# The last 64 keys of an attention chunk: eighth of thirteen slots, one score product, VectorE alone

## The chip, the cores and the metric

The kernel runs on one core of one Trainium2 chip. TensorE (PE in the profile) multiplies, VectorE (DVE), ScalarE (ACT) and GpSimd (POOL) work on elements, and SyncE (SP) issues most DMAs. PEld is TensorE's loading of weights, which overlaps its products. The metric is the time of one execution in device microseconds, the median of three runs.

## The reference

For eight batches of S = 3136 tokens, an attention with squared rectified scores, multiplied by `u`, and then a routed feed-forward layer on 128 tokens of each batch:

```python
scale = 1.0 / S
scores = scale * np.matmul(z, z.transpose(0, 2, 1))     # z: (8, 3136, 64)
attn = np.maximum(scores, 0.0) ** 2
x = u * np.matmul(attn, v)                              # v: (8, 3136, 256)
...
for b in range(B):                                      # routed layer, capacity 128
    top_idx = np.argpartition(-(x[b] @ w_gate), capacity)[:capacity]
    xe = x[b, top_idx]
    ye = np.maximum(xe @ w1, 0.0) @ w2
    out[b, top_idx] = xe + sigmoid(gate)[:, None] * ye
```

## The kernel before

**Precision.** Products run on a reduced form of fp32, so that each operand is kept as a high part, a rounded copy, and a low part, what the rounding left. `ZH` and `ZL` hold the parts of z, with 64 rows of features twice over the 128 partitions; `V` holds both parts of v. `Z[b, c]` is the moving operand of the scores: the high part of a chunk's z on partitions 0 to 63, the low part on the others. So a product with `ZH` and one with `ZL` add up to the full score.

**Chunks and slots.** A batch's queries are cut into seven chunks: five of 512 columns (`c < WHOLE`), one of 256 and one of 320. The keys of a chunk are 24 tiles of 128 and a rest of 64. A slot takes two tiles (a pair), so a chunk has 12 pair slots and one slot for the rest, the thirteenth and last. The list `slots` fixes their order. The scores are symmetric: tiles of squares that an earlier chunk computed are stored transposed to DRAM (`turned` in `low`, tiles `aT`, `squares`) and fetched again (`qk`); such a slot is "old" and needs no score products.

**One slot.** `scores(k)` is issued three slots ahead (`LEAD`): four products of scores for a new pair, into one of two PSUM buffers `sc`. ScalarE rectifies into `a` (L450) and squares into the high part `hi` (L451). The exact square is made on VectorE (L462) or ScalarE (L456), whichever the planner's account (`busy`, `spend`) sees as freer. `low(k)` makes the difference `lo` on VectorE or GpSimd (L518) and, where the tile is wanted later, transposes on VectorE (L483). `mix(k)` then adds twelve products into two PSUM sums `acc` (h = 0 and 1): eight with `hi` and four with `lo`. In the first slot of a chunk they are sorted by sum. Where in the twelve the scores of slot k + 3 are issued is `turn`.

**The rest slot.** The columns of `ZH` and `ZL` behind the 24 tiles hold the last 64 keys twice, so the scores come out twice, on partitions 0 to 63 and 64 to 127. On the lower half `hi` keeps the high part; on the upper half VectorE multiplies (L462, 64x512) and takes the difference (L474). With `hi` holding the high part above the low part, four products with `Vr`, the rest of v twice over, do the whole sum.

**Around a chunk's end.** `finish` queues two readings of the sums on VectorE (L601), transposes and the store of the output. Three PSUM buffers serve the two sums, so the second sum of a new chunk waits for the first reading. The choice of the routed tokens (`route`) and the feed-forward layer (`expert`) of the batch before are cut into tasks that are mixed into later pair slots; on VectorE most of them fall into the second and third chunk of the next batch. In the last batch the last four chunks (`LATE`) are handled by another scheme.

**Order.** Each engine runs its instructions in the order of the program; the schedule is written out by hand.

## Time and profile before

| | |
|---|---|
| median of 3 runs | 2067.78 us (2067.12 to 2067.83) |
| the profiled execution | 2067.41 us |
| its span, first to last instruction | 2065.6 us |
| TensorE busy | 2055.2 us (99%) |
| VectorE, ScalarE, GpSimd busy | 1529.0 us (74%), 1291.2 us (63%), 1357.5 us (66%) |
| granted TensorE clock | 1.0 of full speed |

The median is that of whole executions; the span is measured inside one execution, and some 1.8 us lie around it. Busy times of the engines overlap, so they do not add up to the span. A matmul's busy time in the records covers its whole passage and overlaps the next one; how fast products follow each other is read from their starts.

### The profile page before, as it was taken

The page shows a single profiled execution, that of the slowest core. Times are in us where ns is not written, and L with a number is a line of the kernel's source. Part 1 is how long each engine was busy: PE and PEld are TensorE (multiplying, and loading weights), DVE is VectorE, ACT ScalarE, POOL GpSimd, SP SyncE. Part 2 cuts the span into 40 slices and gives each one's busy share as a digit, 9 for nine tenths or more (in the row PEclk, how much of TensorE's full clock was granted, in tenths as well). Part 3 has the DMA queues.
Part 4 walks back from the last instruction along what each step waited for, and adds up shares of the span by engine and source line. Part 5 has one row for each costly group of instructions (what it writes and reads, how often), then busy time and mean ns, then how long its engine had stood idle before and what let it go on. Part 6 is the DMA issues. An engine that isn't in the chain of part 4 may idle for free.

```text
span 2065.6 us, 31660 instructions
## 1 busy us (share of the span) xinstructions
PE 2055.2 (99%) x10280; PEld 1744.5 (84%) x10280; DVE 1529.0 (74%) x2667; ACT 1291.2 (63%) x1629; POOL 1357.5 (66%) x728
## 2 busy tenths in 40 slices
PE   9999999999999999999999999999999999999999
PEld 6888988889888898888988889888898888888788
DVE  7676678856788667875678756887578876787776
ACT  7665576656775467664676546765477654775543
POOL 6766587756876468764677647875578755765643
PEclk9999999999999999999999999999999999999999
DMA  6788767886668765787767877678776776666862
GB/s 197 207 232 226 217 188 207 233 231 190 193 188 232 212 205 177 199 233 210 208 185 193 235 203 217 184 192 236 194 222 188 192 201 178 206 192 164 213 173 95
DMA packets 442758, 415.52 MB, mean 201 GB/s; under 512 B 133792, under 2 KB 374880, under 8 KB 439520
## 3 DMA queue, kind: packets, MB, share of 16 engines
q1 hardware_dynamic: 441456, 411.01, 70.9%
q0 software_dynamic: 768, 2.10, 0.3%
q8 instruction: 80, 1.31, 0.3%
q14 instruction: 86, 0.70, 0.1%
q10 hardware_dynamic: 368, 0.39, 0.1%
HBM read 238.78 MB, written 174.60 MB: 200 GB/s over the span
## 4 chain that ended last, share of the span: by engine, by line
PE 87%; DVE 3%; issue 2%; ACT 2%; DMA 2%; POOL 1%; SPq 1%; POOLq 0%; DVEq 0%; ACTq 0%
PE acc L556 73%; PE sc L440 12%; ACT hi L451 1%; POOL lo L518 1%; ACT a L450 1%; DVE a L462 1%; DVE aT L483 1%; PE h L1215 1%; PE y L1259 1%; DMA vst<-in_v 0%; DMA squares<-aT 0%; DVE lo L518 0%; DMA qk<-in_zt 0%; PE spread L680 0%; DMA qk<-squares_narrow 0%
## 5 line engine op out<-in xcount | busy, mean ns | idle before, releaser
L556 PE MATMUL acc<-hi,V 128*128 128x512 f32 (+2 forms) x5376 | 1218.4, 364 | 0.5
L518 POOL TENSOR_TENSOR lo<-a,hi 128x1024 fp32r<-128x1024 f32 (+2 forms) x326 | 717.9, 2204 | 563.5 <-DVE a L462 426.7
L556 PEld LDWEIGHTS acc<-hi,V 128*128 128x128 f32 x5376 | 932.9, 188 | 157.4 <-DVE ut L601 5.5
L556 PE MATMUL acc<-lo,V 128*128 128x512 f32 (+2 forms) x2688 | 664.0, 363 | 1.0 <-POOL lo L518 1.0
L450 ACT ACTIVATE a<-sc 128x1024 f32<-128x1024 f32 (+4 forms) x401 | 358.2, 893 | 449.2 <-PE sc L440 421.0
L556 PEld LDWEIGHTS acc<-lo,V 128*128 128x128 f32 x2688 | 471.1, 188 | 76.7 <-POOL lo L518 4.4
L462 DVE TENSOR_TENSOR a<-sc,a 128x1024 f32<-128x1024 f32 (+5 forms) x306 | 307.4, 1005 | 249.8 <-ACT hi L451 225.8
L418 ACT CAST hi<-qk 128x1024 fp32r<-128x1024 f32 (+2 forms) x327 | 279.7, 860 | 220.1 <-PE acc L556 198.1
L483 DVE STREAM_TRANSPOSE aT<-a 128x512 f32<-128x512 f32 (+3 forms) x541 | 349.5, 681 | 76.7 <-ACT a L456 54.4
L451 ACT ACTIVATE hi<-a 128x1024 fp32r<-128x1024 f32 (+4 forms) x401 | 372.2, 928 | 24.8 <-PE acc L556 2.3
L518 DVE TENSOR_TENSOR lo<-qk,hi 128x1024 fp32r<-128x1024 f32 (+2 forms) x220 | 319.2, 1459 | 81.7 <-ACT hi L418 79.3
L440 PE MATMUL sc<-Z,ZH 128*128 128x512 f32 (+2 forms) x746 | 275.1, 373 | 2.3 <-DVE a L462 2.1
L440 PE MATMUL sc<-Z,ZL 128*128 128x512 f32 (+2 forms) x746 | 273.3, 370 | 0.1
L518 POOL TENSOR_TENSOR lo<-qk,hi 128x1024 fp32r<-128x1024 f32 (+2 forms) x107 | 210.0, 1965 | 51.3 <-ACT hi L418 41.6
L440 PEld LDWEIGHTS sc<-Z,ZH 128*128 128x128 f32 x746 | 140.5, 188 | 31.7 <-DVE a L462 6.0
L440 PEld LDWEIGHTS sc<-Z,ZL 128*128 128x128 f32 x746 | 140.5, 188 | 24.7 <-DVE ZL L126 0.5
L126 POOL TENSOR_TENSOR V<-vst,V 128x512 fp32r<-128x512 f32 x92 | 136.5, 1489 | 29.8 <-ACT V L125 26.4
L622 POOL TENSOR_TENSOR ut<-x,w_run 128x1024 f32<-128x1024 f32 (+2 forms) x52 | 126.0, 2422 | 24.4 <-DVE x L613 23.4
L456 ACT ACTIVATE a<-a 128x1024 f32<-128x1024 f32 x93 | 98.8, 1062 | 2.9
L126 POOL TENSOR_TENSOR ZL<-zst,ZH 128x512 fp32r<-128x512 f32 (+2 forms) x56 | 84.2, 1508 | 2.5 <-ACT ZH L125 2.2
L125 ACT CAST V<-vst 128x512 fp32r<-128x512 f32 x95 | 57.9, 609 | 35.5 <-DMA vst<-in_v 35.5
L601 DVE SCALAR_TENSOR_TENSOR ut<-acc,ut 128x512 f32<-128x512 f32 (+2 forms) x112 | 63.9, 611 | 19.5 <-PE acc L556 19.2
(187 smaller groups left out, 1083.1 us busy)
## 6 DMA issues: line engine op xcount, KB each, us to landing
squares<-aT SPq DMA_DIRECT2D x160, 512.0 KB
qk<-squares SPq DMA_DIRECT2D x320, 256.0 KB
squares_narrow<-aT SPq DMA_DIRECT2D x320, 128.0 KB
qk<-squares_narrow SPq DMA_DIRECT2D x80, 512.0 KB
out<-x SPq DMA_DIRECT2D x162, 128.0 KB
ut<-in_ut SPq DMA_DIRECT2D x40, 512.0 KB
vst<-in_v SPq DMA_DIRECT2D x158, 128.0 KB
squares_own<-aT SPq DMA_DIRECT2D x39, 256.0 KB
```

What stands on the lines that cost most here:

```text
L126: (lo_on or nc.vector.tensor_tensor)(lo, src, hi.bitcast(F32), op=ALU.subtract)
L418: nc.scalar.copy(by(hi), src)
L440: nc.tensor.matmul(ps[:, q], z[:, j * P : (j + 1) * P], mov, start=z is ZH, stop=z is ZL)
L450: nc.scalar.activation(a, ps[:, :n], AF.Relu)
L451: nc.scalar.activation(pieces[0][0](hi), pieces[0][1], AF.Square)
L456: nc.scalar.activation(a, a, AF.Square)
L462: square = lambda: nc.vector.tensor_tensor(a[rows], of[rows, :n], a[rows], op=ALU.mult)
L483: nc.vector.transpose(to, a[rows, q].rearrange("p (m t a) -> p m t a", m=GT, a=Q))
L518: on.tensor_tensor(view(lo), src, view(hi).bitcast(F32), op=ALU.subtract)
L556: nc.tensor.matmul(ac[h], w, mov, start=first and h not in started, stop=stop)
L601: nc.vector.scalar_tensor_tensor(xT[:, h, :w], acc[b, c][h], SCALE * SCALE, xT[:, h, :w], op0=ALU.mult, op1=ALU.mult)
L622: nc.gpsimd.tensor_tensor(wx, runs, consts["wg_run"].rearrange("p (o r) -> p o r", o=1).broadcast_to([P, NB, RUN]), op=ALU.mult,)
```

## The change

The last 64 keys' slot moves from the end of a chunk to the eighth place (`MIDDLE`), in the chunks that `inside` names: all but the first of a batch, and in the last batch only the second and third, 44 of 56. There the new `rest_scores` is used. For all chunks the columns of the last keys are laid out anew: `ZH` holds their high parts and then their low parts side by side, `ZL` the reverse. One product with `ZH` then gives the high part's score on partitions 0 to 63 and the low part's on 64 to 127; ScalarE copies the latter down, and VectorE adds, rectifies and squares, rounds to `hi` and takes the difference. The products of other chunks still use both. Because a pair's slot is now the last of such a chunk, it stops the accumulation and has its products sorted by sum.

```diff
@@ -106,6 +106,7 @@
     ROUNDS = 32 // BITS
     SHARES = P >> BITS
     SLOTS = NJ // 2 + 1
+    MIDDLE = SLOTS // 2 + 1
 
     const = ctx.enter_context(tc.tile_pool(name="const", bufs=1))
     vpool = ctx.enter_context(tc.tile_pool(name="vpool", bufs=NJ // 2))
@@ -251,7 +252,9 @@
         on = on or (nc.gpsimd.tensor_tensor if b else None)
         split(src, by_rows(ZH, a, m), by_rows(ZL, a, m), hi_on, lo_on=on)
         if m < n:
-            split(staged["z", b, of][:, o + m : o + n], ZH[:, a + m : a + n], ZL[:, a + m : a + n], lo_on=on)
+            e = a + m + 64
+            for q, (hi, lo) in enumerate(((ZH[:, a + m : e], ZL[:, a + m : e]), (ZL[:, e : a + n], ZH[:, e : a + n]))):
+                split(staged["z", b, of][:, o + m + q * 64 :][:, :64], hi, lo, lo_on=on)
         spend(pool=0.65 + 0.0017 * n if b else 0.0)
 
     def bring_z(b, c):
@@ -316,6 +319,10 @@
 
 
 
+    def inside(b, c):
+
+        return c > 0 and c < (NCH if b < B - 1 else NCH - LATE)
+
     slots = []
     for b in range(B):
         for c in range(NCH):
@@ -333,8 +340,9 @@
             if b < B - 1 and c == NCH - 1:
                 place = [1.6 / len(old)]
             both += [(x, 1, js, False) for x, js in zip(place, new)]
-            slots += [(b, c, js, is_old) for _, _, js, is_old in sorted(both)]
-            slots.append((b, c, (NJ,), False))
+            mine = [(b, c, js, is_old) for _, _, js, is_old in sorted(both)]
+            mine.insert(MIDDLE if inside(b, c) else len(mine), (b, c, (NJ,), False))
+            slots += mine
     assert len(slots) == B * NCH * SLOTS
 
     squares = [
@@ -433,6 +441,8 @@
         if is_second(k):
             mov, w = mov.rearrange("p (f x) -> p f x", x=P)[:, :, P // 2 :], w // 2
         ps = ps_s.tile([P, 2, CH], F32, name="sc", tag="sc")[:, :, :w]
+        if n == 1 and inside(b, c):
+            return rest_scores(k, ps[:, 0], mov)
         todo = [(q, j, z) for q, j in enumerate(js) for z in (ZH, ZL)]
         if k < 2:
             todo.sort(key=lambda x: x[2] is ZL)
@@ -463,15 +473,35 @@
             spend(act=2 * act, dve=dve)
         lows.append((k, a, hi, pieces, square))
 
+    def rest_scores(k, ps, mov):
+
+        b, c, js, _ = slots[k]
+        w = CHUNKS[c][1]
+        nc.tensor.matmul(ps, ZH[:, NJ * P :], mov, start=True, stop=True)
+        both = work.tile([P, 2, CH], F32, name="a", tag="a", bufs=3)[:64, :, :w]
+        hi = work.tile([P, 2, CH], F32R, name="hi", tag="hi2", bufs=LEAD)[:, :1, :w]
+        a, s = both[:, 0], both[:, 1]
+        nc.scalar.copy(s, ps[64:])
+        spend(act=0.13 + 0.0008 * w)
+
+        def square():
+            nc.vector.tensor_tensor(s, ps[:64], s, op=ALU.add)
+            nc.vector.scalar_tensor_tensor(a, s, 0.0, s, op0=ALU.max, op1=ALU.mult)
+            nc.vector.tensor_copy(hi[:64, 0], a)
+            spend(dve=0.3 + 0.0026 * w)
+
+        lows.append((k, both[:, :1], hi, [], square))
+
     def low(k, a, hi, pieces, square):
 
         b, c, js, is_old = slots[k]
         c0, w = CHUNKS[c]
         n = len(js)
         lo = None
-        rows = slice(0, P) if n == 2 else slice(64, P)
+        one = n == 1 and inside(b, c)
+        rows = slice(0, P) if n == 2 else slice(0, 64) if one else slice(64, P)
         if n == 1:
-            nc.vector.tensor_tensor(hi[rows], a[rows], hi[rows].bitcast(F32), op=ALU.subtract)
+            nc.vector.tensor_tensor(hi[64:], a[rows], hi[rows].bitcast(F32), op=ALU.subtract)
             spend(dve=0.05 + 0.001 * w)
         def turned():
             if turns(k):
@@ -489,11 +519,11 @@
                     stores.append(lambda: nc.sync.dma_start(to, t.rearrange("p m q x -> p m (q x)")))
                 else:
                     f0 = q0 // 2 * GT if c < WHOLE else 0
-                    for f in range(GT) if n == 2 else (2, 3):
+                    for f in range(GT) if n == 2 else range(2) if one else (2, 3):
                         if n == 2:
                             to = narrow[f0 + f]
                         else:
-                            to = narrow[2 * GT if c < WHOLE else GT, :, :, (f - 2) * x : (f - 1) * x]
+                            to = narrow[2 * GT if c < WHOLE else GT, :, :, f % 2 * x : (f % 2 + 1) * x]
                         src = t[f * Q : (f + 1) * Q, :, :n].rearrange("a m q x -> a m (q x)")
                         stores.append(lambda to=to, src=src: nc.sync.dma_start(to.rearrange("m a x -> a m x"), src))
             elif is_first(k):
@@ -529,15 +559,15 @@
         b, c, js, _ = slots[k]
         assert k in parts
         hi, lo = parts.pop(k)
-        first, last = k % SLOTS == 0, js[0] == NJ
+        first, last, rest = k % SLOTS == 0, k % SLOTS == SLOTS - 1, js[0] == NJ
         if first:
             acc[b, c] = [ps_a.tile([P, CH], F32, name="acc", tag="acc")[:, : CHUNKS[c][1]] for _ in range(NK)]
         ac = acc[b, c]
         todo = []
-        if last:
+        if rest:
             for h in range(NK):
                 for w in range(2):
-                    todo.append((h, V[b, NJ][:, w, h], hi[:, 0], w == 1))
+                    todo.append((h, V[b, NJ][:, w, h], hi[:, 0], last and w == 1))
         else:
             for h in range(NK):
                 for q, j in enumerate(js):
@@ -545,10 +575,10 @@
                         todo.append((h, V[b, j][:, w, h], hi[:, q], False))
             for q, j in enumerate(js):
                 for h in range(NK):
-                    todo.append((h, V[b, j][:, 0, h], lo[:, q], False))
-            if first and (b or c):
+                    todo.append((h, V[b, j][:, 0, h], lo[:, q], last and q == 1))
+            if first and (b or c) or last:
                 todo.sort(key=lambda x: x[0])
-        turn = (6 if c else 4) if first else 4 if last or len(slots[min(k + 1, len(slots) - 1)][2]) == 1 else 8
+        turn = (6 if c else 4) if first else 4 if rest or len(slots[min(k + 1, len(slots) - 1)][2]) == 1 else 8
         done, lead, started = 0, 2, set()
         for n, (h, w, mov, stop) in enumerate(todo):
             if n == turn:
@@ -559,9 +589,9 @@
             for op in beside[done:upto]:
                 op()
             done = max(done, upto)
+        if last:
+            near.extend(finish(b, c))
         if turn == len(todo):
-            if last:
-                near.extend(finish(b, c))
             between()
 
     gate = {}
@@ -1499,7 +1529,7 @@
         now = settle_scores
         posts = [*posts[:half], now, *posts[half:]]
         held_posts = []
-        if k + 2 < len(slots) and len(slots[k + 1][2]) == 1:
+        if k + 2 < len(slots) and len(slots[k + 1][2]) == 1 and not inside(b, c):
 
             now = square_scores if c < WHOLE and (b or c) else settle_scores
             posts, held_posts = [now], [fn for fn in posts if fn is not settle_scores]
@@ -1515,7 +1545,7 @@
         clock += took
         if tasks:
             ready = max(told + 0.5, clock + 2.0)
-        if len(js) == 1 and cap > 0:
+        if k % SLOTS == SLOTS - 1 and cap > 0:
             if c == NCH - 1 - late:
                 far.extend([None, *route(b)])
             elif c >= NCH - late:
```

The order of the instructions shows where this lands. First TensorE in the second chunk of the fourth batch, before: from the two score products of the last keys, which the tenth slot issues, to their own slot at the end of the chunk. `sc` are score products, `acc` the sums; `Vr` marks the slot of the last keys.

```order
L440 MATMUL sc<-Z,ZH 128x512
L440 MATMUL sc<-Z,ZL 128x512
L556 MATMUL acc<-lo,V 128x512 x4
L556 MATMUL acc<-hi,V 128x512 x8
L440 MATMUL sc<-Z,ZH 128x512
L440 MATMUL sc<-Z,ZL 128x512
L440 MATMUL sc<-Z,ZH 128x512
L440 MATMUL sc<-Z,ZL 128x512
L556 MATMUL acc<-lo,V 128x512 x4
L556 MATMUL acc<-hi,V 128x512 x8
L556 MATMUL acc<-lo,V 128x512 x4
L556 MATMUL acc<-hi,Vr 128x512 x4
```

Two products of scores are followed by what is left of one slot, by two more slots and then by the slot of the last keys. The same chunk after the change, from the products of the fifth slot to the slot of the last keys, the eighth:

```order
L586 MATMUL acc<-hi,V 128x512 x8
L480 MATMUL sc<-Z,ZH 128x512
L586 MATMUL acc<-lo,V 128x512 x4
L586 MATMUL acc<-hi,V 128x512 x8
L450 MATMUL sc<-Z,ZH 128x512
L450 MATMUL sc<-Z,ZL 128x512
L450 MATMUL sc<-Z,ZH 128x512
L450 MATMUL sc<-Z,ZL 128x512
L586 MATMUL acc<-lo,V 128x512 x4
L586 MATMUL acc<-hi,V 128x512 x8
L586 MATMUL acc<-lo,V 128x512 x4
L586 MATMUL acc<-hi,Vr 128x512 x4
```

One product stands where two did, three slots ahead of the four products with `Vr`, which now have pair slots on both sides.

VectorE in the same chunk, before: the middle of the chunk, where the fifth slot's work is, with steps of the routing (`ge`, `tot`, `mi`, `base`) between transposes (`aT`) and a difference.

```order
L808 TENSOR_SCALAR ge,own<-gates,least 128x392
L814 STREAM_TRANSPOSE ge<-own 32x32 x4
L483 STREAM_TRANSPOSE aT<-a 128x4x128 x2
L518 TENSOR_TENSOR lo<-qk,hi 128x1024
L631 TENSOR_REDUCE gate<-ut 128x16
L820 TENSOR_REDUCE tot<-ge 32x16
```

Nothing of the last keys stands here; their multiply and difference come at the end of the chunk. After the change, the same place:

```order
L838 TENSOR_SCALAR ge,own<-gates,least 128x392
L844 STREAM_TRANSPOSE ge<-own 32x32 x4
L488 TENSOR_TENSOR a<-sc,a 64x512
L489 SCALAR_TENSOR_TENSOR a<-a 64x512
L490 CAST hi<-a 64x512
L504 TENSOR_TENSOR hi<-a,hi 64x512
L513 STREAM_TRANSPOSE aT<-a 64x4x128
L513 STREAM_TRANSPOSE aT<-a 128x4x128 x2
L661 TENSOR_REDUCE gate<-ut 128x16
```

The four operations on the last keys and their transpose stand in mid-chunk behind the routing's small transposes, and the difference `lo` that stood there is no longer VectorE's.

## Rows read from the trace of the kernel before

**Rows 1.** The page: span, busy time by engine, the chain that ended last.

```profile
span 2065.6 us, 31660 instructions
PE 2055.2 (99%) x10280; PEld 1744.5 (84%) x10280; DVE 1529.0 (74%) x2667; ACT 1291.2 (63%) x1629; POOL 1357.5 (66%) x728
...
PE 87%; DVE 3%; issue 2%; ACT 2%; DMA 2%; POOL 1%; SPq 1%; POOLq 0%; DVEq 0%; ACTq 0%
```

**Rows 2.** Timeline, TensorE, second chunk of batch four: start us, length us, what.

```profile
821.84 1.98 PE L556 MATMUL acc<-hi,V 128*128 128x512 f32 x8
...
829.09 1.98 PE L556 MATMUL acc<-hi,V 128*128 128x512 f32 x8
830.90 0.39 PE L440 MATMUL sc<-Z,ZH 128*128 128x512 f32 x1
...
832.72 1.98 PE L556 MATMUL acc<-hi,V 128*128 128x512 f32 x8
```

**Rows 3.** Timeline, TensorE, in the chunks of 256 and of 320 columns.

```profile
981.98 1.12 PE L556 MATMUL acc<-hi,V 128*128 128x256 f32 x8
...
988.70 0.64 PE L556 MATMUL acc<-lo,V 128*128 128x256 f32 x4
...
1001.39 1.34 PE L556 MATMUL acc<-hi,V 128*128 128x320 f32 x8
...
1004.91 1.34 PE L556 MATMUL acc<-hi,V 128*128 128x320 f32 x8
```

**Rows 4.** Waits of TensorE's weight loads, whole run: us in total, times, longest.

```profile
PEld sc L440 <- DVE a L462: 6.0, 12, 1.6
PEld acc L556 <- DVE ut L601: 5.5, 13, 0.5
PEld acc L556 <- POOL lo L518: 4.4, 12, 1.1
```

**Rows 5.** Windows: second, third and fourth chunk of batch four.

```profile
core 0: us, PE busy (x) PEld busy (x) DVE busy (x) ACT busy (x) POOL busy (x), PEclk, DMA share, GB/s
...
814.57:856.34 41.77, 41.77 (x188) 34.57 (x186) 39.70 (x96) 29.70 (x32) 29.03 (x15) 1.00 0.59 174
856.34:897.79 41.45, 41.45 (x187) 33.88 (x186) 34.60 (x90) 27.38 (x30) 30.60 (x15) 1.00 0.70 190
897.79:939.90 42.11, 42.11 (x190) 34.79 (x189) 26.69 (x37) 23.43 (x28) 23.62 (x11) 1.00 0.93 250
```

**Rows 6.** Groups by shape: count, busy us, mean ns of one, idle before.

```profile
L462 DVE TENSOR_TENSOR a<-sc,a 128x1024 f32<-128x1024 f32 x186 | 227.3, 1222 | 191.5 <-ACT hi L451 169.3 <-issue 20.9
L518 DVE TENSOR_TENSOR lo<-qk,hi 128x1024 fp32r<-128x1024 f32 x107 | 198.4, 1854 | 14.1 <-ACT hi L418 13.9
...
L474 DVE TENSOR_TENSOR hi<-a,hi 64x512 fp32r<-64x512 f32 x40 | 33.5, 837 | 2.6
...
L462 DVE TENSOR_TENSOR a<-sc,a 64x512 f32<-64x512 f32 x40 | 27.8, 695 | 19.2 <-ACT hi L451 18.1
...
L462 DVE TENSOR_TENSOR a<-a 128x1024 f32<-128x1024 f32 x2 | 2.4, 1222 | 0.4 <-ACT hi L451 0.4
...
L125 DVE CAST ZH<-qk 128x512 fp32r<-128x512 f32 x1 | 0.4, 429 | 0.8 <-DMA qk<-in_zt 0.8
...
L451 ACT ACTIVATE hi<-a 128x512 fp32r<-128x512 f32 x95 | 60.1, 633 | 5.7 <-PE acc L556 0.2
...
L684 ACT COPY row<-spread 128x512 f32<-128x512 f32 x2 | 1.2, 579 | 0.0
```

**Rows 7.** Timeline, VectorE: mid-chunk in the second and third chunk of batch four.

```profile
834.10 0.84 DVE L814 STREAM_TRANSPOSE ge<-own 32x32 f32<-32x32 f32 x4
...
876.87 0.86 DVE L842 TENSOR_SCALAR least<-k_sb,base 32x1 int32<-32x1 int32 x4
878.94 1.23 DVE L462 TENSOR_TENSOR a<-sc,a 128x1024 f32<-128x1024 f32 x1 [1.21 <-ACT hi L451]
```

**Rows 8.** Source L474, the difference for the last keys: ns min/median/max.

```profile
L474 DVE TENSOR_TENSOR hi<-a,hi x56: 422/691/2678, 52.3 to 2037.2; 64x512 fp32r<-64x512 f32 x40, 64x256 fp32r<-64x256 f32 x8, 64x320 fp32r<-64x320 f32 x8
```

## The prediction

> **What bounds the kernel now.** I read the page first. TensorE is busy for 2055.2 of 2065.6 us at the full granted clock, and most of the chain that ended last is its products [rows 1]. A busy TensorE can still lose time between overlapping records, so the next question is the cadence. In the timeline of one chunk (the second of the fourth batch) three slots of 16 products each, all with 512 columns, start at 821.84 and end at 832.72: 10.88 us for 48, so one product costs 0.2267 us when nothing is late [rows 2]. Likewise 56 products with 256 columns take 6.72 us, 0.120 each, and 24 with 320 columns take 3.52 us, 0.147 each [rows 3]. The list of waits says how much of the span is not cadence: weight loads waited 6.0 us for the squares on VectorE, 5.5 for its reading of the sums and 4.4 for a difference on GpSimd, over the whole run [rows 4]. By stage, the windows show TensorE busy without a gap in the chunks around this one, while VectorE is busy for 39.70 of 41.77 us in the second chunk, 34.60 of 41.45 in the third and 26.69 of 42.11 in the fourth [rows 5]. So a product that is taken away is time gained, as long as the engines that feed TensorE stay ahead; VectorE has the least room, in the second chunk of a batch.
>
> **The change part by part.** *The product removed.* In 44 of 56 chunks the last keys need one product where they needed two: 30 chunks of 512 columns, 7 of 256 and 7 of 320 (batches one to seven, all chunks but the first; the last batch, its second and third chunk). The order has exactly that many fewer products with ZL. At the cadences above: 30 x 0.2267 = 6.80, 7 x 0.120 = 0.84, 7 x 0.147 = 1.03, together 8.67 us [rows 2, 3]. This lies on the path, as TensorE waits for almost nothing.
>
> By the Trainium skill (TensorE: Matmul & The Clock Gate, Back-to-back issue gap) an isolated product at full clock takes its columns at 2.4 GHz and 2.5 ns more, 215.8, 109.2 and 135.8 ns here, which would make the sum 8.2 us. The trace's spacing is some 11 ns wider for each, and I use the trace.
>
> *ScalarE* loses a rectification and a square and gets one copy: 0.633 us less for 512 columns, with the copy priced by the copy of another row, 0.579 us [rows 6]. It is not what TensorE waits for; nothing is counted.
>
> *VectorE* did a multiply (0.695 us) and a difference (0.837 us) for these keys. Now it adds (as the multiply, one input still in PSUM: 0.695), rectifies and squares in one instruction, rounds and subtracts. The squaring with both inputs in SBUF lies between half of the in-place square of 1024 columns, 0.61, and the difference's 0.837; I take 0.69. The rounding is like the cast of 128x512, 0.43 [rows 6]. So the chain for 512 columns is 0.695 + 0.69 + 0.43 + 0.837 = 2.65 us where it was 1.53, some 1.1 us more a chunk, at most 44 x 1.1 = 49 us. The planner's own accounts shift too. Counted over the order, 23 squares of pairs go from ScalarE to VectorE (23 x 1.222 = 28 us), and 12 differences of 1024 columns leave it for GpSimd (12 x 1.854 = 22 us) [rows 6]. VectorE's 1529.0 us become about 1585, 77% of the span. In the second chunk of a batch one of those differences leaves, so its load stays near 39.70 + 1.1 + 0.6 - 1.85 = 39.6 us of 41.5. All of this is hidden behind TensorE unless it makes an operand late; then TensorE waits for the difference.
>
> *Is the moved operand late?* In the second chunk, slot 4 (counted from 0) starts at 829.09 [rows 2]. With the new order, slot 4 has 12 products and the one score, 13 x 0.2267 = 2.95 us; slot 5 has 16, 3.63; slot 6 has 12, 2.72: the slot of the last keys starts at 829.09 + 9.30 = 838.39. On VectorE the chain stands right behind the four small transposes that end at 834.94 [rows 7], and the score of these keys is there from 830.9 + 0.4 and copied well before. 834.94 + 2.65 = 837.6, 0.8 us ahead. In the third chunk, slots 4, 5 and 6 before are such that slot 7 comes at 880.4; the last operation ahead of the chain ends at 877.73 with all that stood before it [rows 7], of which one square of 1.22 us is now on ScalarE at that place: 876.5 + 2.65 = 879.2, 1.2 us ahead. The other chunks have VectorE idle for a third of the time. I count 0 for this wait. Its bounds are 0 and, if the two instructions with both inputs in SBUF each took the longest that such a difference took, 2.68 us instead of 0.69 [rows 8], 4.0 - 0.8 = 3.2 us in each of 12 chunks, 38 us. I stay at the near end, since the median of these differences is 0.69 us.
>
> *The end of a chunk* is now a pair's slot, with products sorted by half of the sums. VectorE can read the first sum six products earlier than the end (1.36 us) instead of two (0.45), which can remove up to the 5.5 us of waits for that reading; on the other hand the differences are needed after four products rather than eight, as in the first slot, and the waits for differences there were 4.4 us in all [rows 4]. The bounds are -5.5 and +4.4, and I take 0. Behind the end, the three-slot lead no longer loses a slot of 0.9 us at the boundary, but loses the same in the middle: nothing counted.
>
> *The split of the last 64 keys' z* becomes two pairs of small operations, eight times in the run, on ScalarE and GpSimd, which have a third of their time free [rows 1]. The DMAs are the same in number; those of the last keys' squares leave earlier in the chunk.
>
> The sum: the profiled execution took 2067.41 us for a span of 2065.6; less 8.67 it is 2058.74, with a span of 2056.9. The median of the three runs lies 0.37 us above the profiled one, so the median should be 2067.78 - 8.67 = **2059.1 us**, a gain of 0.42%. About 0.2%, 4.1 us, is what a measurement of this kernel tells from no change.
>
> **The rivals.** *The new chain is held up (slower).* VectorE's square and difference read two SBUF operands while GpSimd works on its 1024-column differences. The rows speak for it: VectorE's difference from two SBUF operands takes 1.854 us for 1024 columns, its multiply with one PSUM operand 1.222 [rows 6], and the difference for the last keys once took 2.678 instead of the usual 0.691 [rows 8]. Against it: that is rare, and before the change the chain ended well ahead. With one such hold (2.0 us, less the 0.8 of slack) in the second and third chunk of batches two to seven, 12 x 1.2 = 14 us are lost: 2073.5 us. It decides from a wait of (8.67 + 4.1) / 12 = 1.06 us a chunk, a chain that is 1.9 us late. In only one of the two chunks it costs 7 us: 2066.3, no change.
>
> The Trainium skill (SBUF — State Buffer, Who interferes with whom) gives a rule of this kind: an instruction of VectorE with two SBUF inputs, or a copy or cast in its two-port mode, and one of GpSimd that reads SBUF shut each other out for a whole instruction. The trace agrees with its direction in the longer durations named; by it the added square and cast could hold GpSimd as well.
>
> *VectorE becomes the bound* in the second and third chunks. For it: 95% busy there [rows 5]. Against it: TensorE shows no gap in that window. If those 12 chunks gain nothing, 12 x 0.2267 = 2.7 us are lost: 2061.8.
>
> *The waits at the chunk ends go as well*: up to 5.5 us more, 2053.6. For it: the earlier last product of the first sum. Against it: part of these waits stands at first chunks of a batch and in the last batch, which keep their order.
>
> *The change does nothing*, the shorter lead in mid-chunk turning all 8.67 us into waits: 2067.8. TensorE's nearly complete lack of waits speaks against it.
>
> **How the numbers follow.** The forecast, 2056.5 to 2061.5, gets 0.68; waits at the ends gone too 0.07; VectorE the bound in some chunks 0.05: faster 0.80. Half or all of the gain lost to a hold in one kind of chunk, or nothing gained, 0.13. The hold in both, 0.07. The range reaches from 2054.5, most of the relief at the ends, to 2064.0, where more than half the gain is gone; about 0.19 lies above it.
>
> **What would show it.** Right: products with ZL down by 44, the span some 8.7 us shorter, all chunks but the first shorter by one product each (41.77 to 41.5 in the second), TensorE's waits in sum within 5 us of before, VectorE near 1585 us and ScalarE lower. The chain of add, square, cast and difference should end before its slot starts. Wrong: waits of TensorE for the difference of the last keys in mid-chunk, above all in the second and third chunk of a batch; VectorE's square or difference at 2 us; new waits for differences in the last slot of a chunk.

## The result, and the profile after

The changed kernel takes 2096.76 us (median of 4 runs, 2095.63 to 2099.92), the kernel before, on the same chip, 2067.81 (2067.12 to 2068.33): a ratio of 1.0143, interval 1.0128 to 1.0158. It is slower by 29 us where the prediction had it faster by 8.7. The profiled execution took 2095.94 us.

The page, with span, engines and chain, to set beside [rows 1]:

```profile
span 2094.2 us, 31433 instructions
PE 2057.2 (98%) x10236; PEld 1736.7 (83%) x10236; DVE 1675.3 (80%) x2783; ACT 1244.6 (59%) x1570; POOL 1355.8 (65%) x731
PE 68%; DVE 14%; DMA 7%; ACT 3%; issue 3%; SPq 2%; POOL 1%; DVEq 0%; POOLq 0%; ACTq 0%
```

The 44 products are gone (10280 to 10236), the span is 28.6 us longer all the same, VectorE works 146 us more, not 56, and its share of the chain that ended last rises from 3% to 14%.

The waits of TensorE, then those of its weight loads (the second list answers [rows 4]; us in total, times, longest):

```profile
PE acc L586 <- DVE hi L504: 10.4, 14, 2.1
PE ahead L925 <- DVE upto L918: 6.0, 5, 1.2
PE sc L450 <- DVE a L472: 3.5, 4, 1.5
PE xeT L1214 <- DMA xe<-out,ids: 2.5, 2, 2.1
```

```profile
PEld acc L586 <- DVE hi L504: 16.9, 20, 2.5
...
PEld acc L586 <- POOL lo L548: 7.2, 20, 1.1
...
PEld acc L586 <- DVE ut L631: 4.3, 11, 0.8
```

Two waits are new: for the difference of the last keys (`hi`, L504), and for the routing's running sums (`upto`, L918). Such a list names only waits for which a releaser was found. A fuller account comes from the starts of the products: what two neighbours lie apart beyond the cadence of the first one's width (0.2267, 0.147, 0.120 us, [rows 2, 3]), summed by what the later one reads; what lies within some 9 ns of the cadence is left out. Worked out so, in us:

```
                            all  last keys  routing  rest parts  rounded parts  scores
before                     26.9     0.9       2.0       3.9          11.7         6.9
after                      63.9    17.9      16.1       7.1          14.4         7.0
e4_move (place alone)      43.9     0.9      13.6       7.3          14.7         6.0
e3_end (scores alone)      41.1     2.4       5.6       3.9          19.6         8.2
e6_shared_mid              60.7     6.8      18.2       7.6          18.6         8.1
e8_squares                 57.6    15.4      11.6       7.4          14.4         7.2
e11_place4                 62.0     0.9      10.8      27.3          15.5         6.1
e12_place10                44.1     1.7       2.8      10.9          14.8        12.4
```

"Rest parts" are products with `lo`, "rounded parts" those of pairs with `hi`; "routing" takes in the products of the feed-forward layer; 1.5 us in each row are of other kinds. The account closes: 63.9 - 26.9 = 37.0 us more waits, less 8.67 for the products, is 28.3, and the span grew by 28.6.

The account holds more than waits. Behind the longest one for the last keys the granted TensorE clock stood at half, 1.2 of 2.4 GHz, for 3.41 us (the 0.50 in the second line, a window), and products of 512 columns lay 0.427 us apart there:

```profile
376.18 2.07 PE L586 MATMUL acc<-hi,Vr 128*128 128x512 f32 x4 [2.07 <-DVE hi L504]
376.21:379.62 3.41, 3.41 (x10) 2.93 (x11) 3.30 (x9) 0.48 (x1) 0.00 (x0) 0.50 0.35 74
```

That is 1.7 us of the account. The kernel before and e4_move have no such stretch ahead of their last microseconds; some other versions have more of them, as will be seen.

By stage: the second and third chunk of batch four, before (first fence) and after, each cut at the first product of the sums:

```profile
814.57:857.25 42.68, 42.68 (x192) 35.32 (x191) 40.61 (x98) 29.70 (x32) 29.94 (x15) 1.00 0.58 171
857.25:897.75 40.50, 40.50 (x182) 33.10 (x181) 33.65 (x88) 27.38 (x30) 29.69 (x15) 1.00 0.71 194
```

```profile
825.00:867.47 42.47, 42.47 (x190) 35.13 (x189) 39.38 (x98) 29.70 (x32) 34.32 (x17) 1.00 0.61 177
867.47:911.04 43.57, 40.92 (x181) 32.65 (x180) 40.50 (x91) 24.89 (x28) 30.61 (x15) 1.00 0.70 185
```

The second chunk is 0.21 us shorter, one product, as forecast. The third is 3.07 us longer: TensorE idles for 2.65 us in it and VectorE's load rose from 33.65 to 40.50 us. Summed over the eight batches by the same cut, the third chunk loses 21.2 us, the first gains 1.6, the second 0.2, the fourth 2.8, and the fifth to seventh lose 5.2, 2.4 and 4.8.

By chunk, 10.7 of the 17.9 us at the last keys' products fall to the third chunks, 0.6 to the second and 6.1 to the two narrow ones.

The timeline shows one chain that ran free (second chunk, batch four) and one that was held (third chunk). VectorE's steps are L488 add, L489 rectify and square, L490 round, L504 difference; the numbers are start and length in us:

```profile
843.38 2.41 POOL L548 TENSOR_TENSOR lo<-a,hi 128x1024 fp32r<-128x1024 f32 x1
845.42 0.68 DVE L488 TENSOR_TENSOR a<-sc,a 64x512 f32<-64x512 f32 x1
846.14 0.68 DVE L489 SCALAR_TENSOR_TENSOR a<-a 64x512 f32<-64x512 f32 x1
846.86 0.42 DVE L490 CAST hi<-a 64x512 fp32r<-64x512 f32 x1
847.31 0.69 DVE L504 TENSOR_TENSOR hi<-a,hi 64x512 fp32r<-64x512 f32 x1
```

```profile
886.80 0.68 DVE L488 TENSOR_TENSOR a<-sc,a 64x512 f32<-64x512 f32 x1
887.46 2.40 POOL L548 TENSOR_TENSOR lo<-qk,hi 128x1024 fp32r<-128x1024 f32 x1
887.51 2.89 DVE L489 SCALAR_TENSOR_TENSOR a<-a 64x512 f32<-64x512 f32 x1
...
890.50 0.42 DVE L490 CAST hi<-a 64x512 fp32r<-64x512 f32 x1
890.96 0.69 DVE L504 TENSOR_TENSOR hi<-a,hi 64x512 fp32r<-64x512 f32 x1
...
891.70 1.20 PE L586 MATMUL acc<-hi,Vr 128*128 128x512 f32 x4 [1.17 <-DVE hi L504]
```

In the second case GpSimd's difference began 0.05 us ahead of the square and ended at 889.86; the square ended 0.54 us behind it, at 890.40. The chain took 4.85 us instead of 2.58, ended 1.28 us behind the time at which TensorE could have started the slot, and the slot waited. In the second chunk it ended 0.84 us ahead of its slot. The add, which reads one operand from PSUM, ran beside GpSimd at its usual 0.68 (845.42, 843.38 + 2.41 = 845.79).

### The profile page after: what moved, and what is told of

Read it like the earlier page. It is cut to its first block, busy times and chain, and to the rows that moved or that the text cites. A ratio compares the mean times of both kernels' runs of the same rounds, so it can differ in the third digit from the quotient of the medians.

```text
span 2094.2 us, 31433 instructions
## 1 busy us (share of the span) xinstructions
PE 2057.2 (98%) x10236; PEld 1736.7 (83%) x10236; DVE 1675.3 (80%) x2783; ACT 1244.6 (59%) x1570; POOL 1355.8 (65%) x731
## 3 DMA queue, kind: packets, MB, share of 16 engines
q8 instruction: 80, 1.31, 0.3%
## 4 chain that ended last, share of the span: by engine, by line
PE 68%; DVE 14%; DMA 7%; ACT 3%; issue 3%; SPq 2%; POOL 1%; DVEq 0%; POOLq 0%; ACTq 0%
PE acc L586 56%; PE sc L450 10%; DVE aT L513 3%; DMA qk<-squares 2%; DVE lo L548 2%; DVE a L472 2%; DMA squares<-aT 2%; DVE a L489 1%; ACT a L460 1%; PE h L1245 1%; ACT hi L461 1%; DMA out<-x 1%; POOL lo L548 1%; PE y L1289 1%; DVE upto L918 1%
## 5 line engine op out<-in xcount | busy, mean ns | idle before, releaser
L548 POOL TENSOR_TENSOR lo<-a,hi 128x1024 fp32r<-128x1024 f32 (+2 forms) x310 | 700.7, 2263 | 567.1 <-DVE a L472 331.2
L460 ACT ACTIVATE a<-sc 128x1024 f32<-128x1024 f32 (+2 forms) x357 | 334.8, 938 | 436.1 <-PE sc L450 390.8
L472 DVE TENSOR_TENSOR a<-sc,a 128x1024 f32<-128x1024 f32 (+3 forms) x285 | 307.1, 1078 | 167.7 <-ACT hi L461 146.9
L548 DVE TENSOR_TENSOR lo<-qk,hi 128x1024 fp32r<-128x1024 f32 (+2 forms) x208 | 303.9, 1469 | 78.7 <-ACT hi L426 72.5
L461 ACT ACTIVATE hi<-a 128x1024 fp32r<-128x1024 f32 (+2 forms) x357 | 347.6, 974 | 21.5 <-PE acc L586 1.3
L548 POOL TENSOR_TENSOR lo<-qk,hi 128x1024 fp32r<-128x1024 f32 (+2 forms) x119 | 239.2, 2012 | 46.0 <-ACT hi L426 32.5
L450 PE MATMUL sc<-Z,ZH 128*128 128x512 f32 (+1 forms) x702 | 258.0, 372 | 4.0 <-DVE a L472 3.5
L450 PE MATMUL sc<-Z,ZL 128*128 128x512 f32 (+1 forms) x702 | 257.8, 371 | 0.1
L466 ACT ACTIVATE a<-a 128x1024 f32<-128x1024 f32 x70 | 74.4, 1063 | 2.2
```

Source lines behind the costliest of these rows:

```text
L450: nc.tensor.matmul(ps[:, q], z[:, j * P : (j + 1) * P], mov, start=z is ZH, stop=z is ZL)
L460: nc.scalar.activation(a, ps[:, :n], AF.Relu)
L461: nc.scalar.activation(pieces[0][0](hi), pieces[0][1], AF.Square)
L466: nc.scalar.activation(a, a, AF.Square)
L472: square = lambda: nc.vector.tensor_tensor(a[rows], of[rows, :n], a[rows], op=ALU.mult)
L548: on.tensor_tensor(view(lo), src, view(hi).bitcast(F32), op=ALU.subtract)
```

## The experiments

Eighteen kernels were run. A ratio is to the kernel before on the same chip, with its interval; "the changed kernel" is 2096.76 us.

### The place alone, and the scores alone

e4_move moves the slot but keeps the old scores, two products and the shared chain (the new layout of z's last keys stays: the two products sum to the same):

```diff
-        if n == 1 and inside(b, c):
-            return rest_scores(k, ps[:, 0], mov)
...
-        one = n == 1 and inside(b, c)
+        one = False
```

> The slot of the last keys in mid-chunk, but their scores as before: two products, rectified and squared on ScalarE, one multiply on VectorE. Nothing of the products is saved. The planner's choices are those of a moved slot (209 squares of pairs on VectorE). Theory L: without the held square no loss, 2062 to 2072 us. Rivals P and M: most of the loss stays, 2088 to 2105 us.

Measured: 2085.45 us, 1.0088 (1.0059 to 1.0117). e3_end is the other half: the new scores with the slot at the end.

```diff
-            mine.insert(MIDDLE if inside(b, c) else len(mine), (b, c, (NJ,), False))
+            mine.append((b, c, (NJ,), False))
...
-        if k + 2 < len(slots) and len(slots[k + 1][2]) == 1 and not inside(b, c):
+        if k + 2 < len(slots) and len(slots[k + 1][2]) == 1:
```

> The new scores of the last keys, but their slot at the end of the chunk as before. Theory L: the square may be held at that place as well, so some waits stay, 2062 to 2075 us. Rivals P and M (the move shifted the planner's squares, or took the lead in mid-chunk): the loss is gone and the removed products show, about 2059 us.

Measured: 2072.55 us, 1.0016 (1.0005 to 1.0028). So the place alone costs some 17 us, all of it waits (43.9 - 26.9 = 17.0), and the scores alone cost 5 instead of gaining 8.67. Together they cost more than the sum: on top of e4_move the scores bring 20.0 us of waits, 17.0 of them at the last keys' products, less 8.67 of products, 11.3 in all.

In e4_move the routing's running sums were held, as in the changed kernel. Its timeline, third chunk of batch four:

```profile
894.91 2.88 DVE L916 TENSOR_TENSOR_SCAN upto<-mk 98x32 bf16<-98x32 bf16 x2
895.34 2.37 POOL L546 TENSOR_TENSOR lo<-qk,hi 128x1024 fp32r<-128x1024 f32 x1
897.85 0.16 PE L923 MATMUL ahead<-upto,c 98*98 98x2 bf16 x1 [0.75 <-DVE upto L916]
```

Before, the two sums took 1.22 us here and nothing waited for them. The first of them had been held there too (1.10 us, ended 0.08 us behind a split of GpSimd), but GpSimd's next instruction came later:

```profile
888.63 1.22 DVE L888 TENSOR_TENSOR_SCAN upto<-mk 98x32 bf16<-98x32 bf16 x2
```

### Is it the held square?

e1_psum leaves the sum in PSUM, so that no step of the chain but the difference has two SBUF inputs; it is one instruction longer:

```diff
-            nc.vector.tensor_tensor(s, ps[:64], s, op=ALU.add)
-            nc.vector.scalar_tensor_tensor(a, s, 0.0, s, op0=ALU.max, op1=ALU.mult)
+            nc.vector.tensor_tensor(ps[:64], ps[:64], s, op=ALU.add)
+            nc.vector.tensor_scalar(a, ps[:64], 0.0, None, op0=ALU.max)
+            nc.vector.tensor_tensor(a, ps[:64], a, op=ALU.mult)
```

> The changed kernel with the sum of the two halves left in PSUM, rectified from there and multiplied PSUM by SBUF: three instructions instead of two for sum, rectification and square, none of which reads two SBUF operands. Theory L (the square, reading two SBUF operands, is held by GpSimd's running instruction: 1.65 us in the mean where 0.68 is free): waits for the last keys' operand fall from some 17 us to under 4, time 2075 to 2082 us. Rival P (the planner's shifted squares overload VectorE in the third chunk): the added 0.6 us an instruction makes no help, 2093 or more. Rival M (the place in mid-chunk alone): as the changed kernel, 2095 or more.

Measured: 2098.83 us, 1.0153 (1.0123 to 1.0182). The groups by shape, of the changed kernel and of e1_psum (count | busy us, mean ns; the 40 differences take in ten of chunks that keep the old scores):

```profile
L489 DVE SCALAR_TENSOR_TENSOR a<-a 64x512 f32<-64x512 f32 x30 | 49.6, 1652 | 1.0
...
L504 DVE TENSOR_TENSOR hi<-a,hi 64x512 fp32r<-64x512 f32 x40 | 33.8, 846 | 1.4
L488 DVE TENSOR_TENSOR a<-sc,a 64x512 f32<-64x512 f32 x30 | 20.3, 677 | 0.8 <-ACT a L484 0.4
...
L490 DVE CAST hi<-a 64x512 fp32r<-64x512 f32 x30 | 17.5, 582 | 2.1
```

```profile
L505 DVE TENSOR_TENSOR hi<-a,hi 64x512 fp32r<-64x512 f32 x40 | 37.8, 944 | 1.4
...
L491 DVE CAST hi<-a 64x512 fp32r<-64x512 f32 x30 | 21.2, 706 | 2.1
L489 DVE TENSOR_SCALAR a<-sc 64x512 f32<-64x512 f32 x30 | 20.5, 683 | 2.1
L490 DVE TENSOR_TENSOR a<-sc,a 64x512 f32<-64x512 f32 x30 | 20.5, 683 | 1.0
L488 DVE TENSOR_TENSOR sc<-sc,a 64x512 f32<-64x512 f32 x30 | 20.5, 682 | 0.6 <-ACT a L484 0.4
```

The steps with a PSUM operand are never held, 682 or 683 ns each. But the hold moves on to the round (582 to 706) and, in the 30 chains, to the difference (685 to 818), and the extra step costs the rest: 3.60 us of work for the chain in the changed kernel (677 + 1652 + 582 + 685), 3.57 here (682 + 683 + 683 + 706 + 818). In the third chunks the wait at the last keys halves (10.7 to 5.2 us), in the second it rises from 0.6 to 7.4; 6.1 of these are one slot of batch three, where the round took 2.32 us and the difference 2.70. The held square as the one cause falls; a chain too long for its place stays.

### Is it the planner's engines?

The place alters the planner's accounts, and 23 more squares of pairs stand on VectorE. e8_squares is the changed kernel with the squares where the kernel before had them, e9_move_sq the same for e4_move, e5_planner fixes the squares and all differences:

```diff
-        if n == 2 and (2 <= k < 2 + LEAD or k > 1 and busy["act"] + 3 * act < busy["dve"] + dve + turned):
+        if (b, c, js[0]) in SQUARES_ON_ACT:
```

> The changed kernel, with the planner's choices of engine for every pair's square and difference taken from the kernel before (186 squares on VectorE instead of 209). Theory L: the held square stays, 2085 us or more. Rival P: VectorE is relieved by some 3 us in the third chunk, the waits for the routing there go, 2070 to 2080 us. Rival M: 2095 or more.

Measured: 2110.39 us, 1.0209 (1.0179 to 1.0238).

> The changed kernel with only the pairs' squares put back where the kernel before had them (186 on VectorE instead of 209); the differences stay with the planner's choice. Theory now: two separate losses, of which one is the squares that the moved slot makes the planner give to VectorE, which then delivers the routing's results late (16 us of waits of routing products in the changed kernel, 2 before), and the other the new chain being late for its slot (18 us of waits, 1 before). By it the routing waits fall under 6 us and the chain's stay above 12: 2082 to 2088 us. Rival (the place in mid-chunk costs by itself, whichever engine squares): routing waits stay above 12 us, 2094 or more.

Measured: 2092.62 us, 1.0117 (1.0094 to 1.0139), between the two.

> The moved slot with the old two-product scores, and the pairs' squares where the kernel before had them. Theory (squares): the moved slot alone lost 17.7 us, of which some 12 are waits of routing products; they go, 2070 to 2076 us. Rival (the place by itself): 2083 or more.

Measured: 2085.83 us, 1.0084 (1.0059 to 1.0108): the squares are not what the place costs. In the changed kernel they cost some 4 us at most, and the two intervals overlap. The engines of before put at the new places give the slowest median of all; the waits of e5_planner:

```profile
PE acc L635 <- DVE hi L553: 16.4, 20, 2.2
PE acc L635 <- POOL lo L597: 15.3, 14, 1.8
```

The routing's waits are nearly gone there (3.6 us in the account), but GpSimd's differences come late in their place (26.0 us at products with rest parts, 22.8 at the last keys). The planner had traded one wait for a smaller one.

### A chain shared with ScalarE

e6_shared_mid gives rectifying and the rounded square to ScalarE, VectorE keeps the add, a multiply with one PSUM operand and the difference; e7_shared_end is the same with the slot at the end, in 512-column chunks only.

```diff
+        nc.vector.tensor_tensor(ps[:64], ps[:64], s, op=ALU.add)
...
-            nc.vector.tensor_tensor(s, ps[:64], s, op=ALU.add)
-            nc.vector.scalar_tensor_tensor(a, s, 0.0, s, op0=ALU.max, op1=ALU.mult)
-            nc.vector.tensor_copy(hi[:64, 0], a)
+            nc.scalar.activation(a, ps[:64], AF.Relu)
+            nc.scalar.activation(hi[:64, 0], a, AF.Square)
+            nc.vector.tensor_tensor(a, ps[:64], a, op=ALU.mult)
```

> The changed kernel with the last keys' work shared again: VectorE adds the halves into PSUM, ScalarE rectifies and makes the rounded square, VectorE multiplies PSUM by SBUF and takes the difference; 2.05 us of VectorE in place of 3.76 for 512 columns. Theory (the long chain on VectorE alone makes the slot's operand late): the waits for the last keys fall from 18 us to under 6, 2080 to 2086 us. Rival (the place in mid-chunk leaves no time for any chain that needs the addition): waits stay above 12 us, 2090 or more.

Measured: 2090.89 us, 1.0108 (1.0087 to 1.0129). The waits at the last keys fall from 17.9 to 6.8 us, yet 4.2 come back at pairs' rounded parts, which ScalarE makes (some 1.1 of them is the clock, at half for 6.8 us around a wait of 3.4 us that ended at 1907.5), and the routing's stay.

> One product, but the slot at the end of the chunk, the work shared between ScalarE and VectorE as in the run before this one, and only in the 30 chunks of 512 columns; the others compute two products as before. If the saved products count at all, up to 30 x 0.227 = 6.8 us are gained less 1.2 us that the new split of z costs at the start: 2062 to 2065 us. Rival (any added step on VectorE is paid back in waits): 2067 to 2070 us.

Measured: 2073.62 us, 1.0023 (1.0013 to 1.0033), worse than the rival. With the slot at the end the saved products are lost too, whichever engine does the work.

### Which place?

e11_place4 and e12_place10 are e4_move with the slot fifth and eleventh of thirteen (`MIDDLE = 4`, `MIDDLE = 10` for 7).

> Old scores, the slot of the last keys moved, but to the fifth of thirteen places instead of the eighth. Theory, that the move costs what the routing chain and its neighbours happen to meet on VectorE and GpSimd at that place: the routing waits (13.6 us at the eighth place, 2.0 at the end) change by more than 4 us, and the time by as much, to either side of 2085. Rival, that any place inside the chunk costs the same, because the last slot is then one with 24 products more whose rest parts are late: within 3 us of 2085.

Measured: 2103.55 us, 1.0175 (1.0158 to 1.0192).

> As the run with the fifth place, but the eleventh of thirteen. Theory: the routing chain, which comes early in the third chunk, lies before this place, so its waits go back towards the 2 us of the kernel before, and the time to 2070 to 2078. Rival (any place inside costs the same): within 3 us of 2085.

Measured: 2084.67 us, 1.0081 (1.0064 to 1.0098). At the eleventh place the routing's waits do go (2.8 us), as the theory said, and the time stays, as the rival said: other waits take their place. Both were too simple. The same spacing, summed in us by slot within the chunk (second to seventh chunk of batches two to seven; slots counted from 0, the short slot's waits in brackets), shows where:

```
slot             0    1    2    3    4    5    6     7     8    9    10   11    12
before          3.0  0.1  0.5  0.2  0.5   -   0.1   0.0   1.1  0.9  0.6  0.2  [0.6]
e11_place4      4.9  0.0  0.5   -  [0.6] 0.1 16.7   0.8   0.0  0.9  3.6  9.9   0.5
e4_move         5.0  0.1   -    -   0.6  0.0   -   [0.4]  0.2  6.8  0.7 11.0   0.1
e12_place10     0.3  0.6   -    -   0.5   -   0.1    -    1.0  4.1 [1.2] 8.9   7.6
after           5.0  0.0   -    -   0.5  0.0   -  [16.1]  1.3  4.5  2.4  9.9   0.1
```

Wherever the slot stands, the pair two slots behind it is late (16.7, 6.8, 7.6 us): in e11_place4 all, in e12_place10 nearly all and in e4_move half of it at products with rest parts. The waits of e11_place4 name the engine:

```profile
PE acc L584 <- POOL lo L546: 15.6, 14, 1.7
```

In the next to last slot (11) each of these has another 9 to 11 us: in e4_move 5.9 of them at the running sums of the third chunk, in e12_place10 5.5 at pairs of the 256-column chunk.

### The held running sums

e13_scan_free was to keep GpSimd from working beside the running sums, by giving the difference issued right behind them to VectorE (the list is filled at the end of the steps of the running sums and of the quotas, and emptied by the next pair):

```diff
-                if busy["pool"] + took > busy["dve"] + dve + (1.2 if busy["pool"] > 0 else 0.0):
+                if beside_scan or busy["pool"] + took > busy["dve"] + dve + (1.2 if busy["pool"] > 0 else 0.0):
...
+            beside_scan.append(1)
```

> Old scores, slot in the eighth place, and the difference of a pair that is issued right behind the routing's running sums, and behind its quotas, is always given to VectorE, so that GpSimd doesn't run beside them (13 differences more on VectorE, some 16 us more work there). Theory, that the routing's VectorE steps are held until GpSimd's difference ends and TensorE waits for them: the waits at the running sums' product (5.0 us) and at the positions' product (1.5) go away, the two running sums take under 0.8 us instead of 2.9, the time falls by 5 to 9 us to 2076 to 2080. Rival, that VectorE is simply late with them at this place: they wait as before, 2083 us or more.

Measured: 2084.55 us, 1.0080 (1.0063 to 1.0097). The edit missed its first aim: the difference that ran beside the sums had been issued ahead of them, so it stayed on GpSimd and the sums still took 2.88 us (third chunk, batch four):

```profile
894.33 2.88 DVE L918 TENSOR_TENSOR_SCAN upto<-mk 98x32 bf16<-98x32 bf16 x2
894.75 2.38 POOL L546 TENSOR_TENSOR lo<-qk,hi 128x1024 fp32r<-128x1024 f32 x1
```

The quotas behind were freed, and nothing was gained by it. What the held sums cost by themselves stays open.

### The rules that went with the place

Inside a chunk the change switches off one rule (the slot ahead of the last keys puts its other work off) and adds one (a pair that is last orders its products by sum). e14_defer restores the first in e4_move, e15_unsorted takes the second out, e16_both does both, e17_after_defer restores the first in the changed kernel.

```diff
-        if k + 2 < len(slots) and len(slots[k + 1][2]) == 1 and not inside(b, c):
+        if k + 2 < len(slots) and len(slots[k + 1][2]) == 1:
```

```diff
-            if first and (b or c) or last:
+            if first and (b or c):
```

> Old scores, slot in the eighth place, and the rule kept that the change switched off inside the chunk: the slot ahead of the last keys issues only the squares at its own end and puts the rest of its VectorE and GpSimd work off to the next slot. Theory, that without the rule this work stands ahead of the operands that are wanted behind the short slot: 15 squares fewer land on VectorE, waits fall from 43.9 to about 30 us, time 2070 to 2076. Rival, that the rule doesn't matter inside the chunk: 2083 us or more.

Measured: 2095.83 us, 1.0135 (1.0117 to 1.0153).

> Old scores, slot in the eighth place, and the last slot of a chunk, now a pair, takes its products in the order of the other pairs (all with the rounded parts first, then those with the rest parts). Theory, that the sorted order wants the rest parts 8 products (1.8 us) earlier: waits at products with rest parts go from 7.3 to 4 us, and the next chunk's start from 0 back to 4 to 5 us, in sum no more than 3 us either way, 2083 to 2088. Rival, that this order is what the place costs: 2075 us or less.

Measured: 2085.58 us, 1.0087 (1.0070 to 1.0104), as e4_move.

> Both edits together: the put-off rule kept, and the last slot in the order of the other pairs. If they add, the time is that of the first run plus the difference of the second to 2085.5; if the rule alone carries it, 2070 to 2076 as there; if neither does, 2083 or more.

Measured: 2097.10 us, 1.0141 (1.0124 to 1.0158): the first plus the second.

> The changed kernel with the put-off rule kept. Theory, that the rule is worth the same here as with the old scores: 10 to 15 us less than 2096.8, 2082 to 2087. Rival, that the late operand of the last keys (17.9 us of waits) and the squares that are held decide here: 2092 us or more.

Measured: 2106.24 us, 1.0186 (1.0161 to 1.0211). The order of the last slot is free; the rule that was switched off had to be. With it the expert's products wait, which they hardly do without. Waits of e14_defer, then two windows of it:

```profile
PE h L1243 <- DVE xs L127: 10.0, 5, 2.2
```

```profile
683.06:686.47 3.41, 3.41 (x10) 2.64 (x9) 3.38 (x4) 0.00 (x0) 2.37 (x1) 0.50 1.05 208
1457.89:1461.30 3.41, 3.41 (x10) 2.64 (x9) 3.37 (x3) 0.75 (x1) 2.29 (x1) 0.50 1.05 231
```

The larger part of that loss is the clock. e14_defer has three stretches at half the granted clock, 13.6 us together, each beside a wait of TensorE of 2.3 to 3.0 us; by the spacing of the products they cost 6.1 of the 10.4 us that it takes over e4_move. In e17_after_defer six such stretches, each beside a wait of 2.0 to 3.2 us, cost 9.9 us, where the one of the changed kernel costs 1.7.

### What is left at the chunk's end

e10_end_wide is e3_end with the new scores in the 512-column chunks alone (`WHOLE` for `NCH` in `inside`):

> New scores on the changed VectorE chain, last slot of the chunk as before, only in the 512-column chunks (the 320- and 256-column chunks keep the two products and the shared chain). Theory, that the new scores with the slot at the end lose in the 320-column chunk because the changed chain stands there: the 8.4 us which that chunk lost in the version with all chunks go away, 29 slots x 4 products less at 0.227 give 6 us at most, 2063 to 2067 us. Rival, that the shorter last slot takes time from the operands that come behind it whichever chain is used: 2069 to 2074 us, with the waits at products with the rounded and rest parts some 8 to 12 us over those of the kernel before.

Measured: 2070.18 us, 1.0014 (1.0004 to 1.0023). (30 slots lose one product each, 6.8 us; the "29 slots x 4" of the expectation is a slip.) The last chunk still loses 3.1 us, though its own slot is as before: of the 8.4 that it lost in e3_end only 5 came from the narrow chunks' chain (both over the first seven batches).

e18_two_chunks has the slot at the end and the new scores in the second and fourth chunk alone, e19_three_chunks in the second to fourth (`c in (1, 2, 3)`):

```diff
-        return c > 0 and c < (WHOLE if b < B - 1 else NCH - LATE)
+        return c in (1, 3) and (b < B - 1 or c < NCH - LATE)
```

> New scores on the changed VectorE chain, slot at the chunk's end, only in the second and fourth chunk (one product of 0.227 us less in 15 slots, 3.4 us). Theory, that the last chunk's loss (3.1 us in the version with all wide chunks) comes from the fifth chunk's slot, a few slots ahead: 2064 to 2066 us. Rival, that the loads are shifted by any such slot: 2067 us or more.

Measured: 2069.92 us, 1.0011 (1.0002 to 1.0021).

> As the run with two chunks, with the third added (22 or 23 slots, 5 us of products). Theory: the last chunk as before, 2063 to 2066 us, unless the third chunk's own loss (2.4 us of waits there) returns, then 2065 to 2067. Rival, any such slot shifts the loads: 2067 us or more.

Measured: 2074.71 us, 1.0038 (1.0024 to 1.0052). All five versions with the new scores and the slot at the end lose more than the products save; that such a slot shifts the loads elsewhere fits them, but no run singles it out. No version came out faster than the kernel before.

## Why the prediction was wrong

**The product removed** was right: 44 fewer, and chunks in which nothing waits are 0.2 us shorter each.

**"I count 0 for this wait"** (the moved operand) is the first step that failed. The waits at the last keys' products are 17.9 us, 17.0 more than before. It took the near end by the median of the difference; the chain forecast at 2.65 us a chunk takes 3.60 us of work on average, 3.73 from the start of the add to the end of the difference, and 4.85 in the third chunk of batch four. The free case was forecast well: in the second chunk of that batch, where nothing was held, the chain ended 0.84 us ahead of its slot (0.8 forecast). In the third it ended 1.28 us late where 1.2 ahead was forecast, and the square there took 2.2 us more than its free time. The term that was mis-sized is the square: 0.69 forecast, which is its free length (0.683), and 1.652 measured. It is held, and not rarely: of all 44 squares of the run, 31 began while an elementwise instruction of GpSimd was running (15 of the routing's products `ut`, 9 splits, 7 differences), and every one of them ended a fixed time behind GpSimd's end (0.54 us for 512 columns, 0.34 for 320, 0.28 for 256); the 13 others took 0.683 or 0.417. Nor was the hold rare before the change. [rows 8] gives a minimum, a median and a maximum, and the maximum is not the one held case: of those 56 differences 26 began beside an instruction of GpSimd and all of them ended 0.28 to 0.55 us behind it; 24 took longer than their free time, the 13 of 512 columns among them 0.92 to 2.68 us instead of 0.69. One of these, behind the GpSimd difference that held it:

```profile
805.95 2.41 POOL L518 TENSOR_TENSOR lo<-a,hi 128x1024 fp32r<-128x1024 f32 x1 [1.65 <-DVE a L462]
807.90 1.00 DVE L474 TENSOR_TENSOR hi<-a,hi 64x512 fp32r<-64x512 f32 x1
```

The mean of 837 ns in [rows 6], beside the median of 691, was the sign of it. The rule cited from the Trainium skill (SBUF — State Buffer, Who interferes with whom) has this: a step of VectorE with two SBUF inputs and one of GpSimd that reads SBUF shut each other out for a whole instruction. The trace agrees, by the 31 squares just named, and the other way round as well: seven splits of `V` (512 columns) that GpSimd began in the last part of a square or a round took 1.53 to 1.55 us, where the median of its 85 others is 1.31. e1_psum shows that moving the hold off the square is not enough, e6_shared_mid that a shorter chain on VectorE takes 11 us of the wait away, and only 6 of the time.

**"Nothing counted"** for the short slot's new place is the second, and as dear: 17.7 us with the old scores (e4_move), 18 to 37 at three places. It said that the three-slot lead loses in the middle what it lost at the end. The slot table shows that it does not: behind the chunk's end the pair two slots on (slot 1 of the next chunk) waits 0.1 us in sum, behind the short slot in mid-chunk 7 to 17. That those operands are late since the short slot lasts 0.9 us, where a pair's lasts 2.7, and what is prepared in the meantime has that much less time, fits the table; no run changed the lead alone, so it is argued, not shown. Nor is settled why the next to last slot suffers at every place. The two rules of the code that went with the place are excluded (e14_defer, e15_unsorted), and so are the squares' engines (e9_move_sq); the engines of the differences were fixed only together with the squares and with the new scores (e5_planner), so they are not.

**"All of this is hidden"** failed with it: VectorE came to 1675.3 us, 90 over the forecast. By groups of instructions, the last keys' steps brought 92 us more where at most 49 were counted: 66.8 for the squares and 28.6 for the rounding, less 3.5 at the differences. The pairs' squares brought the 28 that were counted. The count of the differences was incomplete: 12 of 1024 columns left VectorE (15.1 us less) and 7 of 640 columns (4.5 less), but 23 of 512 columns came to it (26.4 us more), so that the differences brought 7 us where 22 were taken off. Two of the routing's steps, the running sums and the 98x1 steps that write `ahead`, were longer by 20 us in sum, and TensorE waited: of the routing's 16.1 us of waits (2.0 before) 7.0 are at the product behind the running sums. The forecast of VectorE's load in the second chunk held (39.6 us, 39.38 measured); it broke in the third (33.65 to 40.50 us).

**The end of the chunk**, counted 0 with a bound of -5.5, moved to the good side by little: the weight loads' wait for VectorE's reading of the sums went from 5.5 to 4.3 us, and the first chunks gained 1.6 in sum. *ScalarE* fell as forecast. *The split of z*, counted 0, is not free at the very start: the first chunk of batch one is 1.2 us longer, at its scores, and so it is, by 1.0 to 1.2, in e1_psum, e3_end, e4_move, e6_shared_mid and e7_shared_end, which all have the new layout (no run was made without it).

**The rivals.** The held chain was the right one, with the right sign and 2073.5 us, 23 short: it let the hold fall on the last keys alone. Its 14 us of waits are near the 17.9 measured there, in part by luck: it had them in the second and third chunks alike, and they came in the third and the narrow ones. The change's two halves do not simply add up: e3_end and e4_move cost 4.8 and 17.7 us, together 22.5, and both at once 29.

## What to carry to other kernels

Where TensorE has no gap, a product saved is worth its cadence only if no producer is asked for its operand sooner; price the place of a short slot by what stands two slots behind it too, not by the slot alone. A VectorE step with two SBUF inputs is to be priced by its free length plus what is left of the GpSimd instruction that runs at that time, read place by place in the timeline, not by the median of the rows before. GpSimd's busy share (65% here) is no guide to how often: 31 of the 44 squares were held, but 11 of the 44 rounds behind them and none of the 44 differences that end these chains, and the same chunk fares alike in one batch after the other (2.67 to 2.90 us in the third chunks of batches three to seven). And the waits may not be the whole price: beside some of the long ones the granted clock fell to half (1.7 us more in the changed kernel, 9.9 in e17_after_defer). And a planner's choices that fit one order can be the worst for another (e5_planner).

## What the runs showed of the hardware

The hold has a fixed end. All 31 squares that began beside GpSimd ended 0.28 to 0.55 us behind its instruction, by their width alone, and up to 2.90 us after their start; running sums of 98x32 in bf16, free at 0.2 us, ended 0.08 us behind it, after up to 2.44 us; the cast of 64x512, free at 0.42, ended 0.28 us behind it, after up to 2.42. VectorE's three steps with an operand in PSUM in e1_psum were never longer than 0.692 us, 132 of 132, though 92 of them began beside the same kinds of GpSimd instruction:

```profile
L488 DVE TENSOR_TENSOR sc<-sc,a x44: 416/678/692, 77.9 to 1923.3; 64x512 f32<-64x512 f32 x30, 64x256 f32<-64x256 f32 x7, 64x320 f32<-64x320 f32 x7
L489 DVE TENSOR_SCALAR a<-sc x44: 416/683/684, 78.6 to 1924.1; 64x512 f32<-64x512 f32 x30, 64x256 f32<-64x256 f32 x7, 64x320 f32<-64x320 f32 x7
L490 DVE TENSOR_TENSOR a<-sc,a x44: 416/682/685, 79.4 to 1924.8; 64x512 f32<-64x512 f32 x30, 64x256 f32<-64x256 f32 x7, 64x320 f32<-64x320 f32 x7
```

The columns are min/median/max in ns of the three steps with a PSUM operand. So a chain is not freed by freeing one step: the next one with SBUF operands takes the hold over (27 of 44 rounds began beside GpSimd there, 11 in the changed kernel).
